# Attention numerators of the first three chunks: one 128-column product per head pair, or one 64-column product per head on each half of the array

## The chip, the cores and the metric

The kernel runs on one core of a Trainium2 chip. The metric is the device time of one execution in microseconds. The core has a matrix engine (PE, with its weight loads shown apart as PEld), a vector engine (DVE), a scalar engine (ACT), a general engine (POOL) and a queue for transfers (SP). Each works through its own list of instructions in order and waits on semaphores of the others.

## The reference

For 8 batches and 8 heads of 576 tokens with head size 64, the reference computes attention with random features, and then a feed-forward layer:

```
q_p, k_p = phi(q*s), phi(k*s)         # phi(x) = exp(x@omega.T - |x|^2/2 - max) / sqrt(128)
kv  = einsum('bhsm,bhsd->bhmd', k_p, v)        # 128 x 64 for each head
z   = sum over tokens of k_p
num = einsum('bhsm,bhmd->bhsd', q_p, kv)       # the numerators
den = einsum('bhsm,bhm->bhs', q_p, z) + 1e-06
x   = num/den, heads side by side              # 4608 tokens x 512
h = x @ w_in;  out = (h - tanh(h)) @ w_out     # 512 -> 2048 -> 512
```

## The kernel before

The 4608 tokens are worked in 18 chunks of 256. The 8 heads are four pairs (c = 0 to 3), and the two heads of a pair lie on the partitions 0 to 63 and 64 to 127.

There are two ways to compute the attention. Chunks 0 to 2 and batches 0 and 1 go through a stage called native here: plain float32 products, each of which PE runs in two passes. All later chunks and batches go through a second way with split operands (two float32r parts), which the change doesn't touch. In the native stage the kernel also decodes the 16 weight blocks (`decode`, L428 to L455, on ACT, POOL and DVE), since the feed-forward layer needs them.

`k_unit(b, c)` (L170) makes the features of the keys of one batch and pair, sums the two 128x64 matrices kv of its heads in one PSUM bank `pk`, side by side, and copies them out at L221 and L222. Before, the destination is `kvf[b][c]`, a 128x2x128 tile in which head 0 has columns 0 to 63 and head 1 columns 64 to 127 of its own 128 columns. The other halves are zeros, which L530 to L533 write once at the start for eight such tiles, on POOL. After the copy, L225 to L228 lay out the sums z in the same bank.

`q_unit(ch, c)` (L320) makes the features of the queries, divides them by their denominators (L351 to L360), transposes them on PE (L367), copies them to SBUF (`qt`, L370) and multiplies them by kv at L375:

```
for b, s, e in pieces:
    for h in range(2):
        nc.tensor.matmul(pn[:, s:e], kvf[b][c][:, h], qf[:, h, s:e], start=h == 0, stop=h == 1)
```

Both heads add into the same 128 rows of `pn`; since each weight matrix is half zeros, head 0 fills rows 0 to 63 and head 1 rows 64 to 127. Chunk 2 crosses from batch 0 to batch 1 at token 576, so it has two pieces, of 64 and 192 tokens. So there are 8 units with 2 products, and 4 units with 4, which is 32 products and 64 passes. `x_split` (L409) or L382 reads `pn` afterwards.

Order. The Python loop (L555 to L577) starts units at given ticks (`start`, L535 to L541), and interleaves the decoding and the first feed-forward steps (`step`, L545). The framework then orders each engine's instructions by a simulated timeline of its own (`schedule_with_timeline_sim=True`), so that what stands in an engine's list is not the order of the program; the native loads alone are kept in program order on SP (`load`, L78). When the native pool `a0` is closed (L559), the last three weight blocks are loaded into its place. After that, PE runs the feed-forward layer of all chunks, with the second way of attention for later chunks in between.

Of the kernel before, what the change touches and what calls it, by code (L numbers as in the profile page):

```python
# [8 lines left out]
F32 = mybir.dt.float32  # L9
# [8 lines left out]
B, H, S, D, M = 8, 8, 576, 64, 128  # L18
NT, DM, DFF = B * S, H * D, 2048
P = 128  # L20
NC = DM // P
# [10 lines left out]
def favor_attention_ffn(ctx: ExitStack, tc: tile.TileContext, qT, kT, va, vb, vt, omT, w, out):  # L32
# [11 lines left out]
    nc = tc.nc  # L44
# [4 lines left out]
    sb = ctx.enter_context(tc.tile_pool(name="sb", bufs=1))  # L49
# [3 lines left out]
    def open_pool(name, side="right"):  # L53
        pools[name] = tc.tile_pool(name=name, bufs=1, side=side, reuse_waits="tile")
        return pools[name].__enter__()
# [7 lines left out]
    def bank(kind):  # L63
        tags = mode[kind]
        tags.append(tags.pop(0))
        return tags[-1]

    def att(kind, shape, dtype, name):
        pool, bufs = mode[kind]
        return pool.tile(shape, dtype, tag=kind, name=name, bufs=bufs)  # L70
# [7 lines left out]
    def load(dst, src):  # L78

        i = nc.sync.dma_start(dst, src)  # L80
        if mode.get("chain"):
            tc.keep_in_program_order(i)
# [11 lines left out]
    a0 = open_pool("a0")  # L94
# [18 lines left out]
    def kv_tiles(pool, names):  # L113

        ts = [pool.tile([P, 10, E], F32, name=f"v{i}") for i in names]
        ks = [pool.tile([P, P], F32, name=f"kd{i}") for i in names]
        for t, k in zip(ts, ks):
            nc.gpsimd.memset(k, 0.0)
            nc.gpsimd.memset(t[:, :, D:], 1.0)
            for h in range(2):  # L120
                nc.gpsimd.memset(t[D - D * h : P - D * h, 4 + h], 0.0)
        return ts, ks
# [30 lines left out]
    def features_f(f, toks, name):  # L153

        n = 2 * len(toks)
        ph = att("phi", [P, 4, M], F32, f"phi_{name}")
        nb = sb.tile([P, 4], F32, tag="nb", name=f"nb_{name}", bufs=12)
        pj = ps.tile([P, 4, M], F32, tag=bank("pj"), name=f"pj_{name}")
        for i, (a, b) in enumerate(toks):
            nc.tensor.matmul(pj[:, 2 * i : 2 * i + 2].rearrange("p a m -> p (a m)"), f[:, a:b],  # L160
                             om_bd.rearrange("p a m -> p (a m)"), start=True, stop=True)
        nc.vector.tensor_reduce(nb[:, :n], pj[:, :n], axis=AX.X, op=ALU.min)
        for j in range(n):
            nc.scalar.activation(ph[:, j], pj[:, j], AF.Exp, bias=nb[:, j : j + 1], scale=-1.0)
        return ph

    kvf = {}
    kvs = {}

    def k_unit(b, c):  # L170

        n = f"{b}_{c}"
        if not mode["native"]:
            f = att("kf", [P, S], F32, f"kf_{n}")
            load(f, kT[c, :, b * S : (b + 1) * S])
            yield from k_single(b, c, f)
            return
        f = att("kf", [P, 4 * P], F32, f"kf_{n}")
        load(f, kT[c, :, b * S : b * S + 4 * P])
        if (b, c) == (0, 0):  # L180
            fetch(0)
        v, kd = bank("v"), bank("kd")
        halves = [slice(0, D), slice(D, P)]
        for r in halves:
            load(kd[r, r], kT[c, r, b * S + 4 * P : (b + 1) * S])
        load(v[:, 0:4, 0:D], va[b, c, 0])
        load(v[:, 6:10, 0:D], va[b, c, 1])
        for h, r in enumerate(halves):
            load(v[r, 4 + h, 0:D], vb[b, c, r])
        yield  # L190
        phs = []
        for t in range(0, 4, 2):
            phs.append(features_f(f, [(t * P, t * P + P), (t * P + P, t * P + 2 * P)], f"k{t}_{n}"))
            yield
        ph = att("ph5", [P, M], F32, f"ph5_{n}")
        nb = sb.tile([P, 4], F32, tag="nb", name=f"nb5_{n}", bufs=12)
        pj = ps.tile([P, M], F32, tag=bank("pj"), name=f"pj5_{n}")
        nc.tensor.matmul(pj, kd, oms, start=True, stop=True)
        nc.vector.tensor_reduce(nb[:, 0:1], pj, axis=AX.X, op=ALU.min)
        nc.scalar.activation(ph, pj, AF.Exp, bias=nb[:, 0:1], scale=-1.0)  # L200
        yield
        pk = ps.tile([P, 512], F32, tag=bank("pk"), name=f"pk_{n}")
        nc.tensor.matmul(pk[:, 0 : 2 * E], ph, v[:, 4:6].rearrange("p h e -> p (h e)"),
                         start=True, stop=False)
        for h in range(2):
            for t in range(4):
                nc.tensor.matmul(pk[:, E * h : E * h + E], phs[t // 2][:, 2 * (t % 2) + h],
                                 v[:, 6 * h + t], start=False, stop=(h, t) == (1, 3))
            if h == 0:
                yield  # L210

        pkh = pk[:, 0 : 2 * E].rearrange("p (h x) -> p h x", h=2)
        z = sb.tile([P, 2], F32, tag="z", name=f"z_{n}", bufs=4)
        nc.vector.tensor_copy(z, pkh[:, :, D])
        w = None
        if b > 0:
            w = att("kvw", [P, 4, D], F32R, f"kvw_{n}")
            nc.scalar.copy(w[:, 0::3, :], pkh[:, :, 0:D])
            nc.vector.tensor_sub(w[:, 1:3, :], pkh[:, :, 0:D], w[:, 0::3, :].bitcast(F32))
            w = w.rearrange("p a d -> p (a d)")  # L220
        for h in range(2):  # L221
            nc.scalar.copy(kvf[b][c][:, h, D * h : D * h + D], pkh[:, h, 0:D])  # L222
        yield
        for h in range(2):
            nc.tensor.transpose(pk[:, 256 + 128 * h : 384 + 128 * h],  # L225
                                z[:, h : h + 1].to_broadcast([P, P]), ident)
        zb = att("zb0" if b == 0 else "zb", [P, 2, M], F32, f"zb_{n}")
        nc.scalar.copy(zb.rearrange("p h m -> p (h m)"), pk[:, 256:512])  # L228
        kvs[b, c] = (w, zb)
# [90 lines left out]
    def q_unit(ch, c):  # L320

        n = f"{ch}_{c}"
        t0 = ch * TC
        pieces = []
        t = t0
        while t < t0 + TC:
            e = min((t // S + 1) * S, t0 + TC)
            pieces.append((t // S, t - t0, e - t0))
            t = e
        f = att("qf", [P, TC], F32, f"qf_{n}")  # L330
# [13 lines left out]
        for h in range(2):  # L344
            for t in range(2):
                i = ix(h, t)
                for b, s, e in pieces:
                    s, e = max(s, t * P), min(e, (t + 1) * P)
# [6 lines left out]
        for i in range(4):  # L355
            e = bank("norm")
# [11 lines left out]
        if native:  # L368
            qf = att("qt", [P, 2, TC], F32, f"qt_{n}")
            nc.scalar.copy(qf.rearrange("p h t -> p (h t)"), pt)  # L370
            yield
            pn = ps.tile([P, TC], F32, tag=bank("pt"), name=f"pn_{n}")
            for b, s, e in pieces:
                for h in range(2):
                    nc.tensor.matmul(pn[:, s:e], kvf[b][c][:, h], qf[:, h, s:e], start=h == 0, stop=h == 1)  # L375
            if ch == 2:
                if c < 2:
                    x2[c] = sb.tile([P, TC], F32, tag="xs", name=f"x2_{c}", bufs=2)
                elif c == 2:
                    x2[3] = sb.tile([P, DM], F32, tag="o", name="x2")  # L380
                    x2[2], x2[3] = x2[3][:, 0:TC], x2[3][:, TC:]
                nc.scalar.copy(x2[c], pn)  # L382
            else:
                x_split(ch, c, pn, nc.vector)
            xdone[ch] = xdone.get(ch, 0) + 1
            return
# [6 lines left out]
        pn = ps.tile([P, 2, TC], F32, tag=bank("pt"), name=f"pn_{n}")  # L393
# [15 lines left out]
    def x_split(ch, c, x, engine):  # L409
        nc.scalar.copy(xh[:, ch % 2, c], x)  # L410
        engine.tensor_sub(xl[:, ch % 2, c], x, xh[:, ch % 2, c].bitcast(F32))  # L411
# [11 lines left out]
    def fetch(f):  # L423
        if f in places and f not in raws:
            raws[f] = places[f].tile([P, 2 * DM], U64, tag=f"w{f}", name=f"raw{f}")
            load(raws[f], w[f])
# [88 lines left out]
    def tick(new=(), force=False):  # L515
# [7 lines left out]

    weight_places(open_pool("w0", "left"), range(13))
    mode.update(
        chain=True, kvw=(sb, 7), zb=(sb, 6), zb0=(a0, 4), phi=(a0, 4), ph5=(a0, 2), qf=(a0, 2), qt=(a0, 2),
        kf=(a0, 3), native=True, junk=[junk, a0.tile([P, M], F32, name="junk1")],
        norm=[nc.vector,nc.scalar], pj=["pj0", "pj1", "po0", "po1"], pk=["pk", "h0"],
        pt=["pt", "h1"], h=["h0", "h1"])
    for b in range(2):  # L530
        kvf[b] = [a0.tile([P, 2, P], F32, name=f"kvf{b}{c}") for c in range(NC)]
        for t in kvf[b]:
            nc.gpsimd.memset(t, 0.0)  # L533
    mode["v"], mode["kd"] = kv_tiles(a0, (0, 1, 2))
    start = {}  # L535
    for c in range(NC):
# [5 lines left out]
    t = decoded = done = 0  # L542
# [12 lines left out]
    while decoded < NF:  # L555
# [27 lines left out]
        chain=False, native=False, norm=[nc.vector, nc.vector, nc.vector, nc.scalar], junk=[junk],  # L583
        hi=nc.scalar, pj=["pj0"], pk=["pk"], pt=["pj0"],
        phi=(ak, 3), qh=(ak, 1), ql=(ak, 1), tmp=(ak, 1), kf=(ak, 1), kx=(ak, 1), qf=(ak, 2),
# [4 lines left out]
    start = {}  # L590
# [8 lines left out]
    t = 32 - 2 * (NF - done)  # L599
# [67 lines left out]
```

## Time and profile before

| | |
|---|---|
| median of 3 runs | 1079.37 us (1078.85 to 1082.38) |
| the profiled execution | 1079.19 us |
| its span, first to last instruction | 1077.4 us |
| PE busy | 1048.9 us, 97% |
| DVE busy | 851.9 us, 79% |
| ACT busy | 714.4 us, 66% |
| POOL busy | 317.1 us, 29% |
| mean granted PE clock | 0.987 of full |

The ends of matrix instructions are modelled, so PE's busy time has some overlap in it. The spacing from one start to the next tells better what a pass costs.

### The profile page before, as it was taken

The page shows a single profiled execution, that of the slowest core. Times are in us where ns is not written, and L with a number is a line of the kernel's source. Part 1 is how long each engine was busy: PE and PEld are TensorE (multiplying, and loading weights), DVE is VectorE, ACT ScalarE, POOL GpSimd, SP SyncE. Part 2 cuts the span into 40 slices and gives each one's busy share as a digit, 9 for nine tenths or more (in the row PEclk, how much of TensorE's full clock was granted, in tenths as well). Part 3 has the DMA queues.
Part 4 walks back from the last instruction along what each step waited for, and adds up shares of the span by engine and source line. Part 5 has one row for each costly group of instructions (what it writes and reads, how often), then busy time and mean ns, then how long its engine had stood idle before and what let it go on. Part 6 is the DMA issues. An engine that isn't in the chain of part 4 may idle for free. (4 is left out here: it accounts for less than half of the span.)

```text
span 1077.4 us, 20348 instructions
## 1 busy us (share of the span) xinstructions
PE 1048.9 (97%) x6760; PEld 954.1 (89%) x6760; DVE 851.9 (79%) x3028; ACT 714.4 (66%) x1833; POOL 317.1 (29%) x526
## 2 busy tenths in 40 slices
PE   6889999998999999999999999999999999999998
PEld 5777788997999999999999998999999999999997
DVE  6899695798898886688888888898888887666522
ACT  5898564767777675677776766777767775556422
POOL 6333350344433330033333333233333331000000
PEclk8899999998999999999999999999999999999999
DMA  7653300211111110011111111021111110000000
GB/s 249 175 192 130 149 1 17 71 33 52 33 52 33 43 43 20 21 52 33 42 38 33 53 33 50 15 62 33 42 32 48 34 41 11 30 11 26 1 21 20
DMA packets 37194, 55.91 MB, mean 52 GB/s; under 512 B 13921, under 2 KB 23265, under 8 KB 35041
## 3 DMA queue, kind: packets, MB, share of 16 engines
q1 hardware_dynamic: 37008, 54.57, 16.1%
q8 instruction: 54, 0.88, 0.3%
q14 instruction: 52, 0.42, 0.1%
q10 hardware_dynamic: 80, 0.03, 0.0%
HBM read 45.15 MB, written 9.44 MB: 51 GB/s over the span
## 5 line engine op out<-in xcount | busy, mean ns | idle before, releaser
L471 PE MATMUL h<-xh,w 128*128 128x256 f32 (+1 forms) x2176 | 454.0, 292 | 3.1 <-DVE g L476 2.7
L471 PEld LDWEIGHTS h<-xh,w 128*128 128x128 f32 x2176 | 357.0, 191 | 13.3 <-DVE g L476 3.4
L471 PE MATMUL h<-xl,w 128*128 128x256 f32 (+1 forms) x1088 | 317.0, 291 | 0.5 <-DVE xl L411 0.5
L489 PE MATMUL po<-w,gh 128*128 128x512 f32 x544 | 214.3, 394 | 0.0
L471 PEld LDWEIGHTS h<-xl,w 128*128 128x128 f32 x1088 | 207.9, 191 | 6.7 <-DVE xl L411 0.8
L490 PE MATMUL po<-w,gh 128*128 128x512 f32 x544 | 213.7, 393 | 0.0
L491 PE MATMUL po<-w,gl 128*128 128x512 f32 x544 | 209.9, 391 | 0.0
L476 DVE TENSOR_TENSOR g<-h,g 128x512 f32<-128x512 f32 x144 | 98.9, 687 | 65.8 <-ACT g L475 64.9
L475 ACT ACTIVATE g<-h 128x512 f32<-128x512 f32 x144 | 85.2, 591 | 97.8 <-PE h L471 91.2
L477 ACT CAST gh<-g 128x512 fp32r<-128x512 f32 x144 | 89.4, 621 | 88.3 <-DVE g L476 85.3
L478 DVE TENSOR_TENSOR gl<-g,gh 128x512 fp32r<-128x512 f32 x144 | 111.2, 772 | 43.2 <-ACT gh L477 35.9
L491 PEld LDWEIGHTS po<-w,gl 128*128 128x128 f32 x544 | 102.2, 188 | 20.6
L489 PEld LDWEIGHTS po<-w,gh 128*128 128x128 f32 x544 | 102.6, 189 | 16.6 <-ACT gh L477 0.2
L490 PEld LDWEIGHTS po<-w,gh 128*128 128x128 f32 x544 | 102.5, 188 | 15.1
L351 DVE CUSTOM_DVE_ANT_0 junk<-phi_q,zb 128x128 f32<-128x128 f32 (+1 forms) x320 | 96.5, 304 | 15.0 <-ACT phi_q L150 0.8
L442 POOL TENSOR_SCALAR a<-a 128x1024 f32<-128x1024 f32 x16 | 63.7, 3986 | 88.0 <-ACT a L439 85.1
L254 POOL TENSOR_TENSOR khl<-phi_ka,khl 128x256 fp32r<-128x256 f32 x48 | 37.6, 785 | 159.7 <-DVE khl L253 142.3
L150 ACT ACTIVATE phi_q<-phi_q,nb_q 128x128 f32<-128x128 f32 x240 | 79.1, 392 | 4.7 <-DVE nb_q L146 4.3
L262 POOL CAST vhl<-v 128x128 fp32r<-128x128 f32 (+1 forms) x144 | 45.2, 315 | 99.5 <-PE pk L270 80.2
L391 DVE TENSOR_TENSOR ql<-pt,qh 128x512 fp32r<-128x512 f32 x60 | 41.1, 685 | 26.5 <-ACT qh L390 26.2
L146 DVE CUSTOM_DVE_ANT_0 phi_q<-pj_q,phi_q 128x128 f32<-128x128 f32 x240 | 55.8, 284 | 2.8 <-ACT phi_q L143 2.5
L263 DVE TENSOR_TENSOR vhl<-v,vhl 128x128 fp32r<-128x128 f32 (+1 forms) x144 | 44.3, 308 | 16.9 <-POOL vhl L262 13.2
(148 smaller groups left out, 1949.8 us busy)
## 6 DMA issues: line engine op xcount, KB each, us to landing
raw<-w SPq DMA_DIRECT2D x16, 1024.0 KB, 6.3
qf<-qT SPq DMA_DIRECT2D x72, 128.0 KB, 2.1
out<-o SPq DMA_DIRECT2D x36, 256.0 KB, 2.0
kf<-kT SPq DMA_DIRECT2D x24, 288.0 KB, 2.9
v<-vt SPq DMA_DIRECT2D x24, 288.0 KB, 2.9
kf<-kT SPq DMA_DIRECT2D x8, 256.0 KB, 4.1
v<-va SPq DMA_DIRECT2D x16, 128.0 KB, 3.4
kd<-kT SPq DMA_DIRECT2D x16, 16.0 KB, 4.1
```

Source lines behind the costliest of these rows:

```text
L146: nc.vector.tensor_tensor_reduce(ph[:, j], pj[:, i, :M], ph[:, j], scale=-SCALE, scalar=3.0e38, op0=ALU.add, op1=ALU.min, accum_out=nb[:, ...
L150: nc.scalar.activation(ph[:, j], ph[:, j], AF.Exp, bias=nb[:, j : j + 1], scale=-1.0)
L351: nc.vector.tensor_tensor_reduce(bank("junk")[r], ph[r, i], kvs[b, c][1][r, h], scale=1.0, scalar=EPS, op0=ALU.mult, op1=ALU.add, accum_ou ...
L442: nc.gpsimd.tensor_scalar(a.bitcast(F32), a.bitcast(F32), 2.0**-15, 122879.9921875, op0=ALU.max, op1=ALU.min)
L471: nc.tensor.matmul(o, w_, x, start=i == 0, stop=i == len(prods) - 1)
L475: nc.scalar.activation(g, p, AF.Tanh)
L476: nc.vector.tensor_sub(g, p, g)
L477: nc.scalar.copy(gh, g)
L478: nc.vector.tensor_sub(gl, g, gh.bitcast(F32))
L489: nc.tensor.matmul(po[t], h, wt[f][:, 0, DM:], start=first, stop=False)
L490: nc.tensor.matmul(po[t], h, wt[f][:, 1, DM:], start=False, stop=False)
L491: nc.tensor.matmul(po[t], l, wt[f][:, 0, DM:], start=False, stop=last)
```

## The change

kv of a pair becomes one dense 128x2x64 tile, written by one ACT copy instead of two. Each head's product has 64 weight columns and writes only its own 64 rows of `pn`, the lower half for head 0 and the upper for head 1, each product complete in itself. The zero tiles and their eight memsets on POOL are gone. The tiles come from the pool by name, with eight buffers.

```diff
-        for h in range(2):
-            nc.scalar.copy(kvf[b][c][:, h, D * h : D * h + D], pkh[:, h, 0:D])
+        kvf[b, c] = att("kvf", [P, 2, D], F32, f"kvf_{n}")
+        nc.scalar.copy(kvf[b, c], pkh[:, :, 0:D])
...
-                    nc.tensor.matmul(pn[:, s:e], kvf[b][c][:, h], qf[:, h, s:e], start=h == 0, stop=h == 1)
+                    nc.tensor.matmul(pn[h * D : h * D + D, s:e], kvf[b, c][:, h], qf[:, h, s:e],
+                                     start=True, stop=True)
...
-        chain=True, kvw=(sb, 7), zb=(sb, 6), zb0=(a0, 4), phi=(a0, 4), ph5=(a0, 2), qf=(a0, 2), qt=(a0, 2),
+        chain=True, kvw=(sb, 7), zb=(sb, 6), zb0=(a0, 4), phi=(a0, 4), ph5=(a0, 2), kvf=(a0, 8), qf=(a0, 2), qt=(a0, 2),
...
-    for b in range(2):
-        kvf[b] = [a0.tile([P, 2, P], F32, name=f"kvf{b}{c}") for c in range(NC)]
-        for t in kvf[b]:
-            nc.gpsimd.memset(t, 0.0)
```

## Rows read from the trace of the kernel before

**Rows 1.** Page, part 2: the span in 40 equal slices, granted clock.
```profile
PE   6889999998999999999999999999999999999998
PEclk8899999998999999999999999999999999999999
```
**Rows 2.** Windows of 10 us (start:end length, PE PEld DVE ACT POOL, clock, DMA).
```profile
10.00:20.00 10.00, 7.53 (x27) 6.84 (x28) 6.19 (x7) 4.94 (x12) 7.21 (x2) 0.53 0.87 296
30.00:40.00 10.00, 9.13 (x47) 8.08 (x46) 7.62 (x20) 5.75 (x19) 3.46 (x1) 0.78 0.59 184
40.00:50.00 10.00, 9.07 (x54) 7.74 (x55) 10.00 (x33) 10.00 (x33) 3.82 (x1) 1.00 0.58 178
100.00:110.00 10.00, 9.22 (x50) 7.78 (x50) 9.84 (x28) 6.86 (x15) 0.88 (x1) 1.00 0.01 2
120.00:130.00 10.00, 10.00 (x46) 8.27 (x45) 7.81 (x10) 5.73 (x8) 7.22 (x2) 1.00 0.59 238
```
**Rows 3.** The numerator products by their source line, L375.
```profile
L375 PEld LDWEIGHTS pn<-qt,kvf x64: 186/190/192, 46.7 to 114.6; 128*128 128x128 f32 x64
L375 PE MATMUL pn<-qt,kvf x64: 218/379/483, 46.7 to 114.7; 128*128 128x256 f32 x32, 128*128 128x64 f32 x16, 128*128 128x192 f32 x16
```
**Rows 4.** Timeline (start, us, engine, what): the first unit's products.
```profile
46.73 1.08 PE L375 MATMUL pn<-qt,kvf 128*128 128x256 f32 x4
```
**Rows 5.** Timeline at the end of the native stage.
```profile
107.51 1.26 PE L375 MATMUL pn<-qt,kvf 128*128 128x64 f32 x8
108.80 0.69 DVE L476 TENSOR_TENSOR g<-h,g 128x512 f32<-128x512 f32 x1
109.55 0.50 PE L471 MATMUL h<-xh,w 128*128 128x512 f32 x1 [0.78 <-DVE g L476]
112.17 0.39 PE L471 MATMUL h<-xh,w 128*128 128x512 f32 x1
112.41 0.60 PE L367 MATMUL pt<-ident,phi_q 128*128 128x128 f32 x4
113.68 1.36 PE L375 MATMUL pn<-qt,kvf 128*128 128x64 f32 x8 [0.68 <-ACT qt L370]
114.75 0.53 PE L489 MATMUL po<-w,gh 128*128 128x512 f32 x1
```
**Rows 6.** The copies of kv, L222, and a 128x128 copy, L218.
```profile
L222 ACT COPY kvf<-pk x16: 207/260/412, 17.7 to 101.7; 128x64 f32<-128x64 f32 x16
  PEld pk L225: 1.0, 1
  PE pk L225: 0.7, 1
...
L218 ACT CAST kvw<-pk x4: 256/314/468, 62.7 to 98.5; 128x128 fp32r<-128x128 f32 x4
```
**Rows 7.** Timeline of the start of the kernel.
```profile
1.12 0.56 POOL L533 MEMSET kvf<- 128x256 f32 x2
1.95 1.57 POOL L533 MEMSET kvf<- 128x256 f32 x6
3.46 0.20 POOL L118 MEMSET kd<- 128x128 f32 x1
3.70 1.12 SPq L80 DMA_DIRECT2D kd<-kT  x2
5.12 2.98 PE L160 MATMUL pj_k<-om_bd,kf 128*128 128x256 f32 x8 [0.29 <-DMA kf<-kT]
12.54 1.13 ACT L439 ACTIVATE a<-raw 128x1024 f32<-128x1024 f32 x1 [0.17 <-DMA raw<-w]
```
**Rows 8.** Windows of 2 us, native stage.
```profile
16.00:18.00 2.00, 2.00 (x7) 1.73 (x7) 0.92 (x3) 1.24 (x3) 1.45 (x1) 0.50 0.70 190
30.00:32.00 2.00, 2.00 (x10) 1.99 (x10) 0.63 (x2) 1.36 (x6) 2.00 (x1) 0.50 0.97 389
```
**Rows 9.** Windows of 5 us around a stall of PE after the native stage.
```profile
245.00:250.00 5.00, 2.86 (x20) 2.41 (x19) 4.62 (x22) 3.81 (x13) 1.84 (x3) 0.95 0.23 79
250.00:255.00 5.00, 4.13 (x17) 3.20 (x16) 4.66 (x20) 4.91 (x13) 2.56 (x9) 0.50 0.15 56
255.00:260.00 5.00, 4.59 (x22) 4.59 (x23) 4.71 (x18) 3.52 (x11) 3.32 (x6) 0.52 0.41 123
```
**Rows 10.** PE's waits from 115 us to the end (us, times, longest).
```profile
PE pj_kb L142 <- DVE nb_km L146: 1.8, 1, 1.8
PE pt L367 <- ACT o L502: 0.7, 1, 0.7
```

## The prediction

> **What bounds the kernel now.** I read the slices of the page first [rows 1]. From the fifth slice on PE is at 8 or 9 tenths nearly everywhere; the first four, some 108 us, are the native stage, and the change touches only that one. So two questions are left: who sets the end of the native stage, and what PE does with a shift of its start into the feed-forward stage.
>
> For the first I read the windows of 10 us [rows 2]. From 40 to 50 us DVE and ACT are busy 10.00 of 10, and from 100 to 110 DVE still has 9.84, while PE's list is filled to 8 or 9 with matrix records whose modelled ends overlap. So DVE, with ACT close behind, sets the pace from about 40 us; the change takes nothing from DVE. Before that it is not so: from 10 to 20 us DVE has only 6.19 and from 30 to 40 only 7.62, and the granted clock of PE is 0.53 and 0.78 there. From 120 to 130 us PE has 10.00 and DVE 7.81: PE is the bound.
>
> For the place where the bound passes from DVE to PE I read the timeline [rows 5]. PE's numerators at 107.51 end, and PE then idles 0.78 us until DVE's g of 108.80 is done. From 109.55 on PE is the last to be ready: feed-forward products, the transposes at 112.41, 0.68 us of waiting for the copy qt, the last numerators at 113.68, and at 114.75 the output products start, from which on PE runs full. What leaves that last piece before 114.75 moves the whole rest of the kernel; what PE saves before 108.80 mostly lengthens its wait for DVE.
>
> **The change part by part.**
>
> *Numerators on PE.* There are 64 passes in 12 units [rows 3]. In a unit of one piece the four passes take 1.08 us with the last one's 0.379 in it [rows 3, 4], so the spacing is (1.08 - 0.379) / 3 = 0.234 us, and a unit costs 4 x 0.234 = 0.93 us. After the change there are as many passes with as many moving columns; only the weights are narrower. So the gain is whatever runs side by side on the two halves of the array. No row shows a product of 64 columns. At the best head 1 runs wholly beside head 0: half, -0.47 us a unit. In list order a pass can only run beside the one before it when that is of the other head: of the four passes of a unit (head 0 twice, head 1 twice) one is hidden, -0.23 us. At the worst nothing is hidden and PE empties itself before and after; the nearest row for that is what a pass lasts beyond its spacing, 0.379 - 0.234 = 0.145 us, twice, +0.29 us a unit. I take the middle one, since PE's list is in order.
>
> For the last unit, which alone lies on the path: its eight passes run from 113.68 to 114.75, 1.07 us [rows 5]. In list order the columns of the passes are 64, 64 (head 0), 64, 64 (head 1), then 192 four times in the same way; beside their forerunner run the third, the fifth and the seventh, worth 64 + 64 + 192 = 320 of 1024 columns, 31%. That is **-0.33 us** (from -0.53 to +0.29).
>
> The other 11 units lie beside DVE's work: **0**. Were that cover gone, they would be worth 11 x -0.23 = -2.6 us, at the worst 11 x 0.29 = +3.2 us. At 107.51 the saving only makes the 0.78 us wait longer, and what is late next there is DVE's g [rows 5].
>
> A rule of the Trainium skill speaks against this part. What the trace has nearest to it: PE goes from feed-forward products at 112.17 to the transposes at 112.41, 0.24 us later, the normal spacing of such a product, so this change of kind costs nothing to be seen [rows 5]. The Trainium skill, TensorEngine Tiling (Array Packing), section Key Properties, says that a change of the tiling mode empties the engine, while tiles within a mode run independently. No row here shows a tiled product, so neither half is borne out yet. By the rule the emptying would come twice a unit.
>
> *The copy of kv on ACT.* 16 copies of 128x64 with a median of 0.260 us become 8 of 128x128, for which the nearest row is the cast of the same bank at 0.314 median, 0.256 at the least [rows 6]. Counted one by one that is 16 x 0.260 - 8 x 0.314 = -1.6 us of ACT time, less where the two overlapped. ACT is covered by DVE where both are full. What comes through is the wait of PE's z transposes for the second copy, 0.7 us at one place by PE's row [rows 6]; one copy of the two falls away before it. As PE is not the bound there I take **-0.1** (from -1.6 to 0).
>
> *The zero fill on POOL.* Eight memsets, 0.56 + 1.57 us from 1.12 to 3.52 [rows 7], go. They stand ahead of the fill of kd (3.46), and SP's load into kd (3.70) waits behind that, with all later loads, in program order, behind it on SP. So SP can be up to 3.70 - 1.57 = 2.1 us earlier there, if its loads before are through. PE's first product waits for kf, which is issued before all that [rows 7], so it stays at 5.12. What a later load was seen to hold up is ACT at 12.54, 0.17 us for a weight block [rows 7]. I take that: **-0.17** (from -2.1 to 0); the fill itself was hidden behind the transfer of kf.
>
> *Tile space.* Dense tiles are half as large. Nothing in the rows waits for that, but the places of other tiles move, and with them which of them a late weight block waits for: 0, hidden behind the feed-forward steps that run full from 114.75.
>
> The sum: -0.33 - 0.1 - 0.17 = -0.6 us. Against the profiled execution of 1079.19 us that is **1078.6 us**. The median of the runs is 1079.37, 0.18 more, so it is a fair base. All best ends, with the cover gone: -0.53 - 11 x 0.47 - 1.6 - 2.1 = -9.4; all worst: 12 x 0.29 = +3.5. Neither is near: DVE's list is unchanged.
>
> **The rivals.**
>
> *B: the halves don't run side by side, or emptying the array eats what they give.* That is the change not doing what it says. For it: no row shows such a product, and the rule above. Price: at the last unit between 0 and +0.29 us, and the other two terms stay, so 1078.9 to 1079.2; as PE has its idle stretch at 108.8, the other units don't show.
>
> *C: a stretch of half clock or of idle goes.* The order of each list is planned by simulated times, and the simulated times of POOL's start, ACT's copies and PE's products all change; so lists can come out in another order in the native stage and behind it. Two places are worth something. In the native stage PE works full 2 us windows at 0.50, 1.2 GHz, while DVE has 0.92 and 0.63 of 2 [rows 8]; DVE's idle time is 3.8 us from 10 to 20 and 2.4 from 30 to 40 [rows 2]. If one block goes, DVE gains 2 to 3 us. Behind it, PE idles 2.14 + 0.87 + 0.41 = 3.4 us from 245 to 260, and as its clock falls to 0.50 there, the 4.13 + 4.59 us that it works count about half, which is 4.4 us [rows 9]; a DVE result 1.8 us late begins the long part [rows 10]. Whole: -7.8 us. I price C at half of that, -4: 1075. Against it: the tail of the kernel hardly sees the change except as a shift, and PE's idle time there comes from DVE's load.
>
> *D: the other sign by the same planner.* A new order puts a DVE result behind other work once more, where PE has nothing to run, as at 249.3 us [rows 10]. Priced by that same stall, half to whole: +3.9 to +7.8, so 1083 to 1087, 1084 the likelier. It decides from the point where PE's pause is followed by a clock of 0.50, as here; a pause of 0.78 us [rows 5] cost nothing but itself. For it: DVE has 4.6 to 4.7 of 5 us in those windows [rows 9], so there is little room. Against it: there is one such stall only behind the native stage, the next longest kind of wait of PE there is 0.7 us [rows 10].
>
> **How the numbers follow.** The forecast 0.44, B 0.12, C 0.26, D 0.18. Between two versions of this kernel 0.3%, 3.2 us, is about what can be told from no change. The forecast and B lie within it; C lies beyond it in all but its smallest cases, and D in all. So faster 0.26, same 0.56, slower 0.18. The range has to reach into C and D: 1074 to 1083 leaves out the larger half of each, some 0.2. The forecast's own range, with its terms at their ends but the cover kept, is 1077 to 1079.5.
>
> **What would show it.** If the numerators do run side by side, the starts of the four passes of a unit span less than 3 x 0.234 us, and the last unit takes about 0.74 us from its first pass to the output products behind it. If the skill's rule holds in full, gaps stand before the first of them and behind the last. The start is right if SP's loads into kd leave 1 to 2 us earlier and PE's first product still starts near 5.1. DVE's windows from 40 to 110 should stay at 9.6 or more. The output products should start 0.3 to 1 us before 114.75, and the rest should be the rows of before, shifted, with the same stall at 245 to 260. I am wrong if DVE's idle time in the native stage differs by more than 1 us, if that stall goes or a second one comes, or if numerators with 64 columns have passes longer than those with 128.

## The result

| | median | ratio to before, 95% interval |
|---|---|---|
| before | 1080.20 us (1078.85 to 1082.38, 6 runs) | |
| after | 1085.51 us (1083.62 to 1088.65, 6 runs) | 1.0049 [1.0032, 1.0066] |

The change makes the kernel slower by 5 us, 0.5%, where 1078.6 with a range of 1074 to 1083 was forecast. The profiled execution after took 1085.81 us, its span is 1083.9, its mean granted clock 0.980 (0.987 before). Two runs of the later rounds, of 1869 and 2069 us, are left out of all ratios.

### The profile page after: what moved, and what is told of

It reads as the page before. It is cut to its first block, busy times and chain, and to the rows that moved or that the text cites. A ratio compares the mean times of both kernels' runs of the same rounds, so it can differ in the third digit from the quotient of the medians.

```text
span 1083.9 us, 20312 instructions
## 1 busy us (share of the span) xinstructions
PE 1049.3 (97%) x6760; PEld 949.6 (88%) x6760; DVE 850.1 (78%) x3028; ACT 713.4 (66%) x1825; POOL 315.4 (29%) x518
## 5 line engine op out<-in xcount | busy, mean ns | idle before, releaser
L477 DVE TENSOR_TENSOR g<-h,g 128x512 f32<-128x512 f32 x144 | 98.8, 686 | 67.9 <-ACT g L476 67.0
L476 ACT ACTIVATE g<-h 128x512 f32<-128x512 f32 x144 | 85.1, 591 | 101.4 <-PE h L472 93.1
L351 DVE CUSTOM_DVE_ANT_0 junk<-phi_q,zb 128x128 f32<-128x128 f32 (+1 forms) x320 | 94.0, 297 | 14.4 <-ACT phi_q L150 0.5
```

What stands on the lines that cost most here:

```text
L351: nc.vector.tensor_tensor_reduce(bank("junk")[r], ph[r, i], kvs[b, c][1][r, h], scale=1.0, scalar=EPS, op0=ALU.mult, op1=ALU.add, accum_ou ...
L476: nc.scalar.activation(g, p, AF.Tanh)
L477: nc.vector.tensor_sub(g, p, g)
```

## The profile after

In the listings the lines from 376 on stand one higher than before (L476 is now L477); L375, L222, L228 and L367 are the same.

The products first, by their source line, as in [rows 3] (minimum, median, maximum in ns; first and last start):

```profile
L375 PEld LDWEIGHTS pn<-qt,kvf x64: 132/136/232, 46.7 to 121.5; 128*64 128x64 f32 x64
L375 PE MATMUL pn<-qt,kvf x64: 222/354/686, 46.7 to 121.7; 128*64 128x256 f32 x32, 128*64 128x64 f32 x16, 128*64 128x192 f32 x16
```

And on the timeline (start, us), the first unit, as in [rows 4], and the end of the native stage, as in [rows 5]:

```profile
46.74 0.65 PE L375 MATMUL pn<-qt,kvf 128*64 128x256 f32 x4
47.32 0.92 PE L160 MATMUL pj_q<-om_bd,qf 128*128 128x256 f32 x3
...
103.71 0.65 PE L367 MATMUL pt<-ident,phi_q 128*128 128x128 f32 x4 [2.02 <-DVE phi_q L360]
105.89 0.51 PE L472 MATMUL h<-xh,w 128*128 128x512 f32 x1 [1.52 <-DVE g L477]
106.23 0.58 PE L472 MATMUL h<-xl,w 128*128 128x512 f32 x1
106.61 1.05 PE L472 MATMUL h<-xh,w 128*128 128x512 f32 x2
...
121.37 0.66 PE L375 MATMUL pn<-qt,kvf 128*64 128x64 f32 x8
121.96 0.50 PE L490 MATMUL po<-w,gh 128*128 128x512 f32 x1
```

The two heads do run side by side. The next product follows 0.58 us after the first numerator, where a unit cost 0.93; the last unit takes 121.96 - 121.37 = 0.59 us instead of 1.07. But that last unit starts at 121.37, and before it started at 113.68 [rows 5]. The output products start 7.2 us late (121.96 against 114.75), and from there to the end both kernels take the same: 1079.19 - 114.75 = 964.4 us, and 1085.81 - 121.96 = 963.9. So in these two executions the whole loss is made in the native stage.

Where in it? The windows of 10 us, as in [rows 2] (start:end length, PE PEld DVE ACT POOL, clock, DMA):

```profile
30.00:40.00 10.00, 9.49 (x48) 8.36 (x48) 7.64 (x20) 5.71 (x19) 3.13 (x1) 0.77 0.60 187
40.00:50.00 10.00, 8.90 (x54) 6.95 (x53) 9.07 (x33) 10.00 (x31) 4.41 (x1) 1.00 0.57 182
70.00:80.00 10.00, 8.62 (x38) 6.33 (x37) 7.83 (x22) 5.78 (x18) 0.00 (x0) 0.72 0.33 112
100.00:110.00 10.00, 6.46 (x25) 4.87 (x26) 9.90 (x26) 8.40 (x18) 4.04 (x1) 0.83 0.00 0
```

Up to 40 us they are nearly those of before. From 70 to 80 DVE has only 7.83 and the clock is 0.72; from 100 to 110 PE has only 6.46 and the clock is 0.83. Before, the clock was 1.00 from 40 to 140 us. On the timeline the second place is the two pauses above, 2.02 and 1.52 us; in the 4 us behind them the granted clock is 0.60, most of that time at the lower of its two levels (1.2 instead of 2.4 GHz):

```profile
103.00:105.50 2.50, 0.65 (x4) 0.45 (x4) 2.40 (x12) 2.50 (x8) 2.50 (x1) 1.00 0.00 0
105.50:109.50 4.00, 3.62 (x9) 2.90 (x10) 4.00 (x7) 2.78 (x6) 0.62 (x1) 0.60 0.00 0
```

One more cut is useful, from the first numerators to the first g on DVE, and from there to the output products. Before, and then after:

```profile
46.73:96.69 49.96, 42.38 (x246) 35.54 (x245) 49.10 (x157) 47.42 (x136) 16.29 (x5) 1.00 0.54 193
96.69:114.75 18.06, 15.87 (x83) 13.27 (x83) 15.01 (x39) 10.21 (x22) 3.75 (x1) 1.00 0.00 1
```

```profile
46.74:105.15 58.41, 45.90 (x245) 34.55 (x244) 53.23 (x168) 48.46 (x135) 18.70 (x6) 0.91 0.46 164
105.15:121.96 16.81, 16.07 (x83) 11.85 (x83) 11.52 (x25) 8.60 (x18) 0.97 (x1) 0.90 0.27 100
```

DVE's work is about the same in all, 64.1 and 64.8 us. But 168 of its instructions stand ahead of the first g instead of 157, 4.1 us more work, and it idles 5.2 + 5.3 = 10.5 us instead of 0.9 + 3.0 = 3.9. These 6.6 us of idle DVE are nearly the 7.2, in these two executions. The instructions of each engine are the same but for the edits; their order is not: the framework's planner has put all five lists in another order.

## The experiments

The order can be held fixed: a table gives each engine's instructions by their places in the program, and each instruction is made to follow the one before it in the table. So the changed work can run in the old order, and the old work in the new one. All runs are timed in five rounds beside the kernel before. Runs of one kernel differ by 4 to 11 us from one another, so verdicts come from ratios; the profile is of one execution and is used for the mechanism alone.

**The order or the work.** The first theory is the order. The rival: the shorter products leave PE too little to do, and its clock falls.

```diff
+PLAN = {"PE": <the places in the list of before>, "DVE": ..., "Activation": ..., "Pool": ..., "SP": ...}
...
         favor_attention_ffn(tc, *args, o)
+        replay(tc, nc)      # each instruction follows the one before it in PLAN
```

> The changed kernel, but each engine's list is chained in the order that the kernel before has (its one copy of kv stands where the second of the two stood; the zero fills are left out). Theory O (the other order of the lists made it slower): with the old order the time goes back, 1078 to 1080.5 us, no half-clock stretch between 50 and 80 us, the last numerators near 114.5 us. Theory K (the shorter numerators leave PE with too little to do, its clock falls to 1.2 GHz, and PE then is late): the order doesn't matter, 1083 to 1087 us, granted clock under 0.9 in the windows from 50 to 80 us, the last numerators at 119 us or later.

> The kernel before (zero-padded tiles, two copies, eight fills, products of 128 columns), but each engine's list is chained in the order that the changed kernel has. Theory O: as slow as the changed kernel, 1083.5 to 1088 us, since numerators that cost more PE time stand in the same worse order. Theory K: as the kernel before, 1078 to 1081 us, with the clock at 1.00 from 50 to 80 us, since PE has its longer numerators back.

The changed work in the old order: ratio 0.9990 [0.9976, 1.0004]. The old work in the new order: 1.0047 [1.0024, 1.0069], as slow as the changed kernel. At a fixed order the work is worth -0.0010 in the old one and +0.0002 (1.0049 against 1.0047) in the new one, nothing that can be told from zero. The order is the cause; the rival falls, since the shorter products cost nothing in the old order, and the longer ones are as slow as they in the new. The clock can't decide it: in the old order it was 0.83 from 60 to 70 us, where I had expected no half-clock stretch, and 1.00 from 70 to 140.

**Which stretch of the order.** The changed work in the old order, with one section of every list taken from the new order: the middle of the native stage, its end, or all that lies behind it. And then the first two together.

```diff
-PLAN = {"PE": <old order>, ...}
+PLAN = {"PE": <old order, but for places 174 to 308: new order>, ...}   # e4; e3: up to 174; e5: from 308; other lists cut at the same work
```

> The changed work throughout; each engine's list in the order of the kernel before, but for the first part (up to PE's place 174, some 87 us), which stands in the order of the changed kernel. The loss of 5 to 6 us was seen in two places: here, where PE's granted clock fell to 0.72 from 70 to 80 us and the weight blocks came late, and at the end of the native stage. Theory O1, both places count, each for about half: +2 to +4 on the 1079.0 of the same work in the old order, so 1081 to 1083, and a stretch of half clock between 68 and 76 us. Rival O2, the loss is made at the end of the native stage, and the lag in the middle is caught up before it, since DVE is then the pace: 1079 to 1080, with the last numerators near 111 to 114 us. Rival O3, the middle is the whole: 1084 to 1086.

> The changed work; the old order but for the end of the native stage (PE's places 174 to 308, some 87 to 122 us), which stands in the order of the changed kernel. In both kernels that were run in the new order the z layout of unit 1,3 (L228) comes at 109.0 to 113.5 us, and at 100.5 to 103.5 in both that were run in the old one, and the first feed-forward products behind it follow late. Theory O1: +3 to +4, so 1082 to 1083. O2: 1083 to 1086, the whole loss, with z of unit 1,3 from 108 us on and output products from 116 us on. O3: 1079 to 1080.

> The changed work; the old order but for everything behind the native stage (PE's places from 308 to 1092, where the two orders run together again), which stands in the order of the changed kernel, SP's places too. Theories O1 to O3: 0 to +1, so 1079 to 1080, as PE runs full there. Rival O4, the loss stands in the stall of PE at 240 to 280 us: 1082 to 1085, with PE's clock below 0.9 from 260 to 280 us.

> The changed work; the whole native stage in the order of the changed kernel (the middle and the end together), everything behind it in the order of the kernel before. The end alone cost 0.27% (1.0017 against 0.9990), the middle alone nothing, the rest nothing; the changed kernel as it is stands at 1.0049. Theory O5, the native stage's order is all of it, and the middle costs only where the end is in the new order too: ratio 1.004 to 1.006, 1084 to 1086. Rival O6, the parts add up, and the rest of the list counts only together with them: 1.001 to 1.003, 1081 to 1083.

The middle: 0.9987 [0.997, 1.0004]. The end: 1.0017 [1.0002, 1.0032]. The rest: 0.9990 [0.9977, 1.0003]. Middle and end together: 1.0053 [1.0035, 1.0071]. So the native stage's order is all of it (O5); the end costs 0.27% by itself, and the middle costs 0.36% more, but only where the end is in the new order too. By the intervals each of these two differences is uncertain by some 0.2%. O1 was wrong on the middle: the half clock from 70 to 80 us, which I had counted as a loss, was there in the profiled run of the middle as well (0.78), and in a profiled run of the old order (the rest's, 0.65 from 60 to 70 us); by the ratios these two kernels lose nothing by their order.

**Which edit brought the order about.** Two kernels with one edit each, in the planner's own order, and the whole change in the order that came out for the first of them.

```diff
-  nc.tensor.matmul(pn[:, s:e], kvf[b][c][:, h], qf[:, h, s:e], start=h == 0, stop=h == 1)
+  nc.tensor.matmul(pn[h * D : h * D + D, s:e], kvf[b][c][:, h, D * h : D * h + D],
+                   qf[:, h, s:e], start=True, stop=True)                              # e6
...
-  for h in range(2):
-      nc.scalar.copy(kvf[b][c][:, h, D * h : D * h + D], pkh[:, h, 0:D])
+  nc.scalar.copy(kvf[b][c].rearrange("p h (i d) -> p (h i) d", i=2)[:, 0::3, :], pkh[:, :, 0:D])   # e10
```

> The kernel before with one edit of the change alone: each head's product takes 64 weight columns, a slice of its tile half of zeros, and writes its own 64 rows. Two copies, the zero fills and the tiles are as before. The order is the planner's own; its lists lie nearer to those of the changed kernel (160 of PE's places differ) than to those of before (489 differ). If it is the new order that makes the change slower, and the shorter products are what brought the order about: 1083 to 1087. Rival: the order came from the copies and fills that moved, or near likeness of the lists is not enough: 1077 to 1080.

> The kernel before with one edit alone: one ACT copy of 128x128 in place of two of 128x64, into the tile half of zeros; products and fills as before, the order the planner's own (91 of PE's places differ from before, 419 from the changed kernel). I expect 1078 to 1081, no difference; if the single copy itself is bad, or any other order is: 1083 or more.

> The changed work in a third order: that which came out for the half-column products alone (ratio 0.9983). Behind the native stage that order is the same as the changed kernel's. If only the order made the change slower: 1077 to 1079, ratio 0.997 to 0.9995, faster than the changed kernel by 6 to 8 us with every edit of it in. Rival, the single copy and the dropped fills have a price of their own that the old order hid: 1080 to 1083.

The products alone: 0.9983 [0.9973, 0.9993]. The copy alone: 1.0043 [1.0026, 1.0061]. The whole change in the third order: 0.9996 [0.9981, 1.0012]. Both of my guesses by likeness of the lists were wrong. The products alone, whose list is nearest to the slow one, are the only version that beats the kernel before, by 1.8 us; the copy alone, with 91 of PE's 6584 places moved, by the traces all at the end of the native stage (from 78 us on), loses about as much as the whole change. In the old order the same copy, beside the rest of the change, costs nothing that can be seen (e1). The whole change in the third order came out between my two ranges, so by its interval the single copy and the dropped fills may still cost some 0.1%. No edit accounts for the 0.5%; two of the four orders that the planner made are bad.

The kernel before was not run with its own order held fixed. What the holding itself does to the time is seen only where an order was run both ways: the products alone in the planner's order at 0.9983 and the whole change in the same order, held, at 0.9996; the changed kernel at 1.0049 and with its native stage held at 1.0053. These differences, 0.13% and 0.04%, are small beside the 0.6% in question.

**What in the order.** The pauses of 2.02 and 1.52 us at the end of the stage looked like rival D of the prediction in another place. I mended them.

```diff
 PLAN["DVE"]:         # the changed kernel's list
-  dn(2,1) complete; w, a of the decode; 1/dn(2,1); ...; m of the decode; phi_q(2,1) x2; ...; g
+  dn(2,1) complete; 1/dn(2,1); phi_q(2,1) x2; w, a of the decode; ...; m of the decode; g; ...
...
 PLAN["Activation"]:
+  phi_q(2,1) x2 ahead of m of the decode; tanh ahead of the exps of unit 2,3
```

> The changed kernel in its own order, with seven instructions of two lists moved forward at the end of the native stage: on DVE the reciprocal (L354) and the two scalings (L360) of unit 2,1 to right behind their last denominator, ahead of three instructions of the weight decode (about 1.2 us each), and the first g (L477) ahead of one reduction, one z copy's follower and the scalings of unit 2,2; on ACT the other two scalings (L358) ahead of a decode instruction, and the first tanh (L476) ahead of four exps. PE's list is untouched. Theory D, a DVE result stands behind other work where PE has nothing to run, and PE's clock halves after the pause: PE's waits of 2.02 us for phi_q and 1.52 us for g shrink to under 1 us each, the half clock behind them goes (some 1.7 us), and the time falls by 2 to 4.5 us, to 1081 to 1083.5 (ratio 1.001 to 1.003). Rival: DVE's total load, not the order of these few, sets the end, and the pause only moves: 1085 to 1086.5.

The ratio was 1.0044 [1.0022, 1.0065] against 1.0049: nothing came back that can be told from zero, and the result lies nearer to the rival's than to the 1.001 to 1.003 of theory D. PE's waits in that stretch (at the start of each line; the wait stands in brackets):

```profile
103.76 0.50 PE L472 MATMUL h<-xh,w 128*128 128x512 f32 x1 [0.69 <-DVE g L477]
109.51 0.50 PE L492 MATMUL po<-w,gl 128*128 128x512 f32 x1 [0.40 <-DVE gl L479]
111.24 0.50 PE L472 MATMUL h<-xh,w 128*128 128x512 f32 x1 [1.00 <-DVE g L477]
```

The pauses shrank from 3.54 to 0.69 us and the half clock behind them went (1.00 from 100 to 110 us), but the DVE work that was moved back now makes PE wait at 109.5 and 111.2, and in this execution the clock was 0.66 from 90 to 100 us, where it was 1.00. The next three runs ask for the DVE work that went ahead of g. By the lists these are nine entries: one decode step, the copy of z, four denominators (the five below are a slip), the reciprocal and two scalings of unit 2,2.

```diff
 PLAN["DVE"]:         # e11: the old list; e13 the reverse, in the changed kernel's list, with eight of the nine
-  ...; g; dn; z; m of the decode; dn x3; 1/dn(2,2); phi_q(2,2) x2; ...
+  ...; dn; z; m of the decode; dn x3; 1/dn(2,2); phi_q(2,2) x2; g; ...
...
-PLAN["PE"]: <old order>
+PLAN["PE"]: <old order, but for places 174 to 308: new order>     # e12, PE's list alone
```

> The changed work in the order of the kernel before (0.9990 there), with one edit in DVE's list: the first g (L477) is put behind the nine instructions that stand ahead of it in the changed kernel's list and not in the old one (a decode step of 1.2 us, the copy of z, five denominators, the reciprocal and two scalings of unit 2,2). With the new order of the whole end of the native stage the ratio was 1.0017, and DVE had 53.6 us of work ahead of the first g instead of 49.9, of which 0.8 us came back behind it. Theory G, it is this DVE work ahead of g: ratio 1.001 to 1.003, +2 to +4 us, and DVE busy some 53 us between the first numerators and g. Rival P, PE's list is what costs: 0.998 to 1.000.

> The changed work in the order of the kernel before, with PE's list alone, and only at the end of the native stage (places 174 to 308), in the order of the changed kernel; DVE and ACT stay in the old order. Theory G: 0.998 to 1.000. Rival P: 1.001 to 1.003.

> The changed kernel in its own order (1.0049), with eight of those nine DVE instructions moved behind the first g, the reciprocal of unit 2,1 to right behind its last denominator, and on ACT the first tanh ahead of four exps. Theory G: the 3 us that the end of the native stage costs go, ratio 1.001 to 1.003; what is left is the half clock in the middle. Rival P, or that DVE's total sets the end wherever g stands: 1.004 to 1.006, as the milder edit of the same place had 1.0044.

The late g in the old order: 1.0017 [1.0002, 1.0033], as much as the whole end of the new order. PE's list alone: 1.0022 [1.0006, 1.0038], about the same. The early g in the new order: 1.0050 [1.0033, 1.0068], no gain; there DVE waits 2.87 us for ACT's tanh ahead of g. Both theories were right in what they add and wrong in what they exclude: either list alone costs 0.3%, the whole end with both costs no more (1.0017), and moving g back alone gains nothing. In the profiled executions it looks like DVE's idle time, in the cut used above (first numerators to g, g to output products). The changed work in the old order, then with the late g, then with PE's list:

```profile
42.65:93.71 51.06, 41.74 (x245) 32.22 (x244) 49.85 (x161) 47.50 (x132) 16.51 (x5) 0.97 0.53 192
93.71:111.29 17.58, 14.59 (x83) 10.83 (x83) 15.00 (x39) 10.11 (x21) 3.76 (x1) 1.00 0.26 99
```

```profile
42.86:99.38 56.52, 41.83 (x245) 32.12 (x244) 55.67 (x174) 48.59 (x134) 19.75 (x6) 0.94 0.51 183
99.38:118.03 18.65, 17.24 (x82) 12.64 (x82) 11.76 (x25) 8.84 (x18) 1.36 (x1) 0.82 0.27 103
```

```profile
46.76:101.45 54.69, 45.81 (x243) 34.06 (x242) 49.41 (x159) 43.73 (x124) 14.97 (x5) 0.91 0.49 177
101.45:121.87 20.42, 16.63 (x84) 12.16 (x84) 15.65 (x39) 13.27 (x28) 4.11 (x1) 0.92 0.26 98
```

In the old order 49.85 us of DVE's work stand ahead of g, 15.00 behind it, and DVE idles 1.2 + 2.6 = 3.8 us. With the late g, 55.67 stand ahead, and PE's longest wait is for it:

```profile
100.11 0.79 PE L472 MATMUL h<-xh,w 128*128 128x512 f32 x1 [5.22 <-DVE g L477]
```

Behind it the clock is 0.82 and DVE, with 11.76 us left, idles 6.9 us beside a PE that has become the bound. With PE's list alone g is early for DVE, but DVE idles 5.3 us ahead of it and 4.8 behind.

But one profile doesn't price an order this way. The kernel with the rest in the new order (e5, 0.9990) has the same native stage as the first of these three (0.9990), list for list, and in its profiled execution DVE idles 4.2 + 3.6 = 7.7 us, as much as with the late g:

```profile
43.65:97.46 53.81, 44.93 (x245) 34.49 (x244) 49.65 (x157) 47.04 (x131) 16.11 (x5) 0.90 0.50 179
97.46:116.07 18.61, 17.20 (x82) 12.65 (x82) 15.04 (x39) 10.12 (x21) 3.76 (x1) 0.82 0.28 104
```

The first of the three was the fastest of its 12 runs (1076.22, median 1079.04), and that with PE's list 2.3 us above its median. So the ratios show that either list costs, and that the price is made of DVE's idle time is not shown.

The third order is the limit of this account. There, too, DVE has more ahead of g (55.05 us, and 54.24 for the products alone), and it costs nothing. The half-column products in that order:

```profile
42.80:97.59 54.79, 44.22 (x245) 33.46 (x244) 54.24 (x175) 48.83 (x141) 16.33 (x6) 0.91 0.50 175
97.59:113.74 16.15, 15.79 (x83) 11.88 (x83) 11.36 (x24) 8.60 (x17) 3.36 (x1) 0.88 0.00 1
```

PE gets through the part behind g in 16.15 us, but that is no reason: in the slow native stage of e7 it took 15.7. So what counts is how the lists fit one another: a late g costs 0.3% in the old order, more work ahead of g costs nothing in the third, and an early g gains nothing in the new one. Why the third order is fast, and why the middle costs 0.36% ahead of the new end and nothing ahead of the old one, is not settled.

## Why the prediction was wrong

*The step that failed* is the sentence that closes the sum: "DVE's list is unchanged", and with it "the rest should be the rows of before, shifted". DVE's instructions are unchanged, and their order is not. The sum priced what each edit adds and removes in the old order, and in the old order the time agrees with it: 0.9990 is -1.1 us [-2.6, +0.4], against a forecast of -0.6, though no change would agree as well. The term that the sum put at nothing, the planner's new order, is +6 us.

*The rival that came true in kind* is D, and the number lies in its range (1083 to 1087). I gave it 0.18. Its mechanism (a DVE result behind other work, a pause of PE, half clock behind it) was seen, but not where I put it. I looked for it behind the native stage, where the list of before had its one long stall [rows 9, 10]; it came at the end of the native stage, at the g whose pause of 0.78 us [rows 5] I had said costs nothing but itself. And the one pause is not the price: mended, it came back elsewhere. That the number lies in D's range is luck, since the range was priced by the stall at 249 us, which did not change the time. C's argument, that all lists can come out in another order, is the same as D's, and I gave the good sign more than the bad one. Of four orders that the planner made, two were 0.4 to 0.7% slower than the other two.

*Numerators.* Right in kind, mis-sized. From its first numerator to the next product a unit takes 0.58 us, -0.35 instead of -0.23, and the last one 0.59, -0.48 instead of -0.33: I had let a pass run only beside the one before it, and the passes of the two heads start in pairs. But part of this is lost at either end of the unit. The first unit with the products around it, before and then after (PEld is the weight load; the product at 47.86 is the second of the four at 47.65):

```profile
46.62 0.28 PE L207 MATMUL pk<-v,phi_k 128*128 128x66 f32 x1
46.73 0.43 PE L375 MATMUL pn<-qt,kvf 128*128 128x256 f32 x1
47.43 0.41 PEld L160 LDWEIGHTS pj_q<-om_bd,qf 128*128 128x128 f32 x2
47.65 1.03 PE L160 MATMUL pj_q<-om_bd,qf 128*128 128x256 f32 x4
47.86 0.38 PE L160 MATMUL pj_q<-om_bd,qf 128*128 128x256 f32 x1
```

```profile
46.53 0.28 PE L207 MATMUL pk<-v,phi_k 128*128 128x66 f32 x1
46.74 0.44 PE L375 MATMUL pn<-qt,kvf 128*64 128x256 f32 x2
47.32 0.73 PEld L160 LDWEIGHTS pj_q<-om_bd,qf 128*128 128x128 f32 x4 [0.39 <-ACT phi_q L358]
47.64 0.38 PE L160 MATMUL pj_q<-om_bd,qf 128*128 128x256 f32 x1
```

The first numerator starts 0.21 us behind the product ahead of it, where it was 0.11. The weights of the next product are loaded only as it starts, at 47.32; before, at 47.43, 0.22 us ahead of it. And the second product behind the unit follows the first by 0.32 us instead of 0.21. Behind the same kinds of product the order makes no difference: the changed work in the old order (e1) has 0.21 and 0.32, the old work in the new order (e2) 0.11 and 0.22. The forecast had such a price, 0.145 us twice, only in its worst case. Over the whole stretch, from the product ahead to that second product, the unit gives 1.24 - 1.11 = 0.13 us and not 0.35. Rival B falls all the same: the halves run side by side, and what is lost at the ends doesn't eat all that they give. The Trainium skill, TensorEngine Tiling (Array Packing), section Key Properties, says that a change of tiling mode empties the engine and that tiles within a mode run independently. The trace agrees with both: some 0.1 us is lost at either end of this unit, and the first passes of both heads start at 46.74.

*The copy of kv.* 8 copies of 0.324 us instead of 16 of 0.260, -1.6 us of ACT's time as worked out; it is not seen in the time.

*The zero fill.* SP's load into kd leaves 1.26 us earlier (2.44 against 3.70), as forecast. That PE's first product stays at 5.12 was wrong, it starts at 4.53:

```profile
2.44 1.19 SPq L80 DMA_DIRECT2D kd<-kT  x2
4.50 1.59 PEld L160 LDWEIGHTS pj_k<-om_bd,kf 128*128 128x128 f32 x8 [0.26 <-POOL oms L111]
4.53 1.97 PE L160 MATMUL pj_k<-om_bd,kf 128*128 128x256 f32 x8
```

Two things are needed for that product. The weights om_bd come from POOL (L107, L108), which stood behind the fills, and are ready at 4.88 before and 3.98 after; I had looked at kf alone. And kf, issued at 1.36 and 1.35, lands 3.6 us later before and 3.0 after; why, no run shows. The 0.59 us are given back: the first numerators start at 46.74, and at 46.73 before [rows 4].

*The stall at 245 to 260 us* is still there, its long wait 2.8 us instead of 1.8 [rows 10]:

```profile
PE pj_kb L142 <- DVE nb_km L146: 2.8, 1, 2.8
```

It makes no difference to the 964 us behind the native stage.

## What to carry to other kernels

Where a planner orders the lists by simulated times, an edit has two prices: its work in the old order, which a profile gives, and a new order, which it doesn't. Ask first whether the edit changes what the planner sees; if so, give the new order a term of its own, of either sign and here as large as 0.5%, before adding up tenths of a microsecond. To tell the two apart, run the new work in the old order, and the old work in the new.

Mending the one pause that the timeline shows need not help where DVE is full on either side of it: look at the idle time of the pacing engine over the whole stage. But take it from several executions: here it was 3.8 and 7.7 us in two runs of one and the same order of the stage, and only the ratios of many runs told the orders apart.

## What was not expected of the hardware

Two float32 products of 64 columns on the two halves of the array save 38% of a unit with equal pieces (0.93 to 0.58 us) and 45% of one with 64 and 192 tokens (1.07 to 0.59), more than a pass beside its forerunner alone would give. At either end of the first unit, between full-width float32 products, some 0.1 us is lost again, so that it gives 0.13 us net. A weight load of 64 columns takes 0.136 us (median) instead of 0.190.

At one and the same order of the native stage (the changed work in the old order, and that with the new rest) the profiled runs have the clock at 0.83 and at 0.65 from 60 to 70 us. Such stretches of half clock come and go between executions, so one in a single profile is no evidence for a cause.
